# Attention by half a batch at a time ahead of and beside the first expert: float32 scores, normalised weights, one table of distances

## The chip, the cores and the metric

The kernel runs on one core of one Trainium2 chip. The metric is the device time of one execution, in microseconds (us), and less is better. Three timed runs of the kernel before took 1486.0, 1486.02 and 1492.36 us; the median is 1486.02 us.

## The reference, cut to what matters

Three layers follow one another, all in float32: attention with 2 batches, 8 heads, 768 positions and 64 elements a head; a mixture of 8 experts (1536 tokens, width 512, hidden width 1024) whose gates are normalised 8 times over rows and columns (the Sinkhorn steps); and a gated layer of hidden width 1536.

```python
def _attn_ref(q, k, v, n_global, n_local):      # n_global = 8, n_local = 96
    scores = scale * np.matmul(q, k.transpose(0, 1, 3, 2))
    rel = pos[:, None] - pos[None, :]
    is_global = pos[None, :] < int(n_global)
    is_local = (rel >= 0) & (rel < int(n_local))
    keep = is_global | is_local
    dist = np.where(is_global & ~is_local, float(n_local), np.abs(rel))
    bias = -slopes[:, None, None] * dist[None, :, :]
    scores = np.where(keep, scores + bias, -1e9)
    scores = scores - np.max(scores, axis=-1, keepdims=True)
    a = np.exp(scores)
    a = a / (np.sum(a, axis=-1, keepdims=True) + 1e-09)
    return np.matmul(a, v)

def _moe_ref(x, w_gate, w1, w2):
    P = np.exp(x @ w_gate - max)
    for _ in range(8):
        P /= P.sum(1, keepdims=True) + 1e-09
        P /= P.sum(0, keepdims=True) + 1e-09
        P *= N / E
    for e in range(E):
        out += P[:, e:e + 1] * (np.maximum(x @ w1[e], 0.0) @ w2[e])
```

## The kernel before, in words

Every large product is made of three products in the type float32r: a number is split into a high part and the rest (`xh` and `xl`, `wh` and `wl`, `hh` and `hl`), and high times high, high times rest and rest times high are added up in PSUM. Splitting a piece of weights takes one copy on ScalarE (L191, the high part) and one subtraction on GpSimd (L192, the rest).

Attention works on an item: one pair of heads and one block of 128 queries, against 256 keys (32 copied global keys, the 96 keys before the block and its own 128). There are 2 batches times 4 pairs times 6 blocks, 48 items. For an item TensorE makes the scores (L853; three float32r products for each head, with the heads in rows 0 to 63 and 64 to 127 of the array), VectorE adds a table of the head's biases and takes the minimum (L865), ScalarE takes the exponential (L870), two items later TensorE transposes the weights (L883) and ScalarE copies them out of PSUM (L884), and one item after that TensorE multiplies them with the values in float32 (L897, L901). The values have a 65th column of ones, so the row sums come out beside the result; VectorE divides by them (L729 to L733), and TensorE transposes the result (L719) into `xh` and `xl`. GpSimd copies the global keys and values into the blocks (L859, L906) and makes the tables of biases (L802, L807).

The program is generated in the order in which each engine runs it. Up to 97.2 us it emits the items of batch 0 (and the first steps of batch 1's), with the split of the first weights beside them. Bfloat16 products of zeros (`fill`, L657) stand ahead of and among the first items. Then come the visits of expert 0. A visit is one quarter of the hidden width, and runs one unit for each chunk of 3 blocks of tokens: the first product (two parts, f = 0 and 1, of 12 matmuls each), and then the second products of the unit before (3 blocks, 6 matmuls each). After each part and each block a tick is called, which emits some steps of a list that is spread evenly over the ticks (`Paced`). In the 4 visits of batch 0, of two units each, the list holds the items of batch 1. In the 4 visits of batch 1 it holds the gates with the 8 Sinkhorn steps, and the sums of halves of x that the experts 1 to 7 need (`trans_steps`). The weights of visit n+1 are split in the last unit of visit n. PSUM banks 2, 3, 6 and 7 are shared in turn by transposes and expert products in the visits of batch 0.

Of the kernel before, what the change touches and what calls it, by code (L numbers as in the profile page):

```python
# [9 lines left out]
F32 = mybir.dt.float32  # L10
F32R = mybir.dt.float32r
# [16 lines left out]
WAIT = 3  # L28
LAG = 2
TURN = (4, 4)  # L30
# [36 lines left out]
def tile_global_local_attention__then__sinkhorn_moe__then__glu(  # L67
# [86 lines left out]
    NB0 = NQ  # L154
    F0 = 2 * NB0
# [49 lines left out]
    def split_steps(n):  # L205

        vis = visits[n]
        steps = []
        if vis["kind"] == "moe":
            if vis["load"]:  # L210
                r = raw[vis["raw"]][:, 0 : 4 * FQ]
                steps += split_halves(r, wh[vis["slot"]][0], wl[vis["slot"]][0])
                steps += second_steps(n)
                steps.append(lambda b=vis["raw"]: load(b))
            return steps
# [11 lines left out]
    def split(n):  # L227
        for step in split_steps(n):
            step()
# [190 lines left out]
    def unit_second(n, t, at, j):  # L420
# [4 lines left out]
        if vis["kind"] != "glu":  # L425
            if n in (0, NB0):
# [184 lines left out]
    with tc.tile_pool(name="attn", bufs=1) as ap:  # L611
# [7 lines left out]
        qr = [ap.tile([P, NB, P], F32, name=f"qr{i}") for i in range(2)]  # L619
        kr = [ap.tile([P, NB, P], F32, name=f"kr{i}") for i in range(2)]  # L620
        vo = [ap.tile([P, NB, 2, D1], F32, name=f"vo{i}") for i in range(2)]

        def load_qk(s, blocks=slice(0, NB)):
            load_heads(s, ((qr, q), (kr, k)), blocks)

        def load_vo(s, blocks=slice(0, NB)):
            load_heads(s, ((vo, v),), blocks)

        def load_heads(s, pairs, blocks):
            if s >= B * NP:  # L630
                return
            b, p = divmod(s, NP)
# [701 lines left out]
```

## Time and profile before

| what | us |
|---|---|
| median of three runs | 1486.02 |
| the profiled execution's own time | 1493.77 |
| its span, from the first to the last instruction | 1492.0 |
| TensorE busy | 1465.4 (98%) |
| VectorE busy | 859.7 (58%) |
| ScalarE busy | 499.6 (33%) |
| GpSimd busy | 523.9 (35%) |
| mean granted TensorE clock | 0.984 |

The span lies 1.8 us inside the execution's own time. Matmuls overlap one another, so a busy TensorE is not a full one: what a group of matmuls costs is read from the starts of what stands in a row. The chain that ended last runs through TensorE for 95% of the span. Of the 40 slices of 37.3 us, the first two show granted clocks of 8 and 7 tenths, and all others 9 tenths or more.

### The profile page before, as it was taken

The page shows a single profiled execution, that of the slowest core. Times are in us where ns is not written, and L with a number is a line of the kernel's source. Part 1 is how long each engine was busy: PE and PEld are TensorE (multiplying, and loading weights), DVE is VectorE, ACT ScalarE, POOL GpSimd, SP SyncE. Part 2 cuts the span into 40 slices and gives each one's busy share as a digit, 9 for nine tenths or more (in the row PEclk, how much of TensorE's full clock was granted, in tenths as well). Part 3 has the DMA queues.
Part 4 walks back from the last instruction along what each step waited for, and adds up shares of the span by engine and source line. Part 5 has one row for each costly group of instructions (what it writes and reads, how often), then busy time and mean ns, then how long its engine had stood idle before and what let it go on. Part 6 is the DMA issues. An engine that isn't in the chain of part 4 may idle for free.

```text
span 1492.0 us, 19772 instructions
## 1 busy us (share of the span) xinstructions
PE 1465.4 (98%) x7427; PEld 1282.4 (86%) x7427; DVE 859.7 (58%) x1587; ACT 499.6 (33%) x1064; POOL 523.9 (35%) x604
## 2 busy tenths in 40 slices
PE   8999998899999999999999999999999999999998
PEld 6888877789998999989999999899998888888887
DVE  4455437867666657666666666667665533333323
ACT  4554422333333333333333333333333331122111
POOL 3312103454444444445345445344452211121110
PEclk8799999999999999999999999999999999999999
DMA  7232100122122122121222122121220100010002
GB/s 163 65 93 57 50 2 21 37 74 90 50 71 72 62 88 71 50 71 58 91 71 71 50 71 99 51 71 50 71 85 29 43 29 29 29 43 29 0 1 85
DMA packets 83605, 87.33 MB, mean 59 GB/s; under 512 B 41264, under 2 KB 58672, under 8 KB 83504
## 3 DMA queue, kind: packets, MB, share of 16 engines
q1 hardware_dynamic: 83216, 86.01, 18.5%
q8 instruction: 59, 0.97, 0.3%
q14 instruction: 42, 0.34, 0.1%
q10 hardware_dynamic: 288, 0.00, 0.0%
HBM read 73.42 MB, written 12.58 MB: 58 GB/s over the span
## 4 chain that ended last, share of the span: by engine, by line
PE 95%; DVE 2%; POOL 1%; issue 1%; ACT 1%; DMA 1%; SPq 0%; DVEq 0%; ACTq 0%; POOLq 0%
PE bank L354 29%; PE bank L356 29%; PE bank L355 29%; PE bank L853 2%; PE bank L901 1%; PE bank L883 1%; PE bank L897 1%; PE bank L708 1%; POOL wl L192 0%; PE bank L719 0%; DMA work<-in_moe_w_gate_dram 0%; PE bank L1282 0%; DMA lens<-in_n_local_dram 0%; DVE work L1122 0%; DVE csum L1207 0%
## 5 line engine op out<-in xcount | busy, mean ns | idle before, releaser
L437 DVE SCALAR_TENSOR_TENSOR acc<-bank,gate,acc 128x512 f32<-128x512 f32 x336 | 251.8, 749 | 232.9 <-PE bank L356 230.0
L354 PE MATMUL bank<-wh,hh 128*128 128x512 f32 x912 | 360.8, 396 | 0.0
L356 PE MATMUL bank<-wh,hl 128*128 128x512 f32 x912 | 360.0, 395 | 0.0
L355 PE MATMUL bank<-wl,hh 128*128 128x512 f32 x912 | 358.2, 393 | 0.0
L192 POOL TENSOR_TENSOR wl<-raw,wh 128x512 fp32r<-128x512 f32 (+1 forms) x188 | 201.8, 1089 | 378.4 <-ACT wh L191 370.3
L354 PE MATMUL bank<-xh,wh 128*128 128x384 f32 (+1 forms) x720 | 255.5, 355 | 5.4 <-DVE kept L539 3.0
L356 PE MATMUL bank<-xh,wl 128*128 128x384 f32 (+1 forms) x720 | 252.9, 351 | 0.0
L355 PE MATMUL bank<-xl,wh 128*128 128x384 f32 (+1 forms) x720 | 251.7, 350 | 0.0
L356 PEld LDWEIGHTS bank<-wh,hl 128*128 128x128 f32 x912 | 171.4, 188 | 38.7
L354 PEld LDWEIGHTS bank<-wh,hh 128*128 128x128 f32 x912 | 171.7, 188 | 27.2
L355 PEld LDWEIGHTS bank<-wl,hh 128*128 128x128 f32 x912 | 171.6, 188 | 26.7
L529 ACT ACTIVATE hh<-kept 128x384 fp32r<-128x384 f32 x168 | 88.1, 525 | 314.5 <-DVE kept L539 314.5
L354 PEld LDWEIGHTS bank<-xh,wh 128*128 128x128 f32 x720 | 137.0, 190 | 19.2 <-DVE kept L539 3.3
L355 PEld LDWEIGHTS bank<-xl,wh 128*128 128x128 f32 x720 | 136.8, 190 | 13.4 <-DVE xl L1287 0.5
L356 PEld LDWEIGHTS bank<-xh,wl 128*128 128x128 f32 x720 | 136.3, 189 | 5.7
L192 POOL TENSOR_TENSOR wl<-work,wh 128x256 fp32r<-128x256 f32 x112 | 93.4, 835 | 94.3 <-ACT wh L191 94.3
L543 ACT ACTIVATE kept<-bank 128x384 f32<-128x384 f32 x168 | 82.4, 491 | 122.7 <-PE bank L356 122.7
L531 DVE SCALAR_TENSOR_TENSOR hl<-kept,hh 128x384 fp32r<-128x384 f32 x168 | 115.3, 687 | 0.4 <-ACT hh L529 0.3
L356 PE MATMUL bank<-th,wl 128*128 128x384 f32 x336 | 113.0, 336 | 0.0
L354 PE MATMUL bank<-th,wh 128*128 128x384 f32 x336 | 112.5, 335 | 0.1
L355 PE MATMUL bank<-tl,wh 128*128 128x384 f32 x336 | 112.4, 335 | 0.0
L412 DVE TENSOR_TENSOR z<-bank,sg 128x512 f32<-128x512 f32 x36 | 24.9, 692 | 139.3 <-PE bank L356 139.3
(151 smaller groups left out, 1908.9 us busy)
## 6 DMA issues: line engine op xcount, KB each, us to landing
raw<-in_moe_w_dram SPq DMA_DIRECT2D x68, 512.0 KB, 4.3
glw<-work SPq DMA_DIRECT2D x36, 256.0 KB, 2.3
raw<-glw SPq DMA_DIRECT2D x18, 512.0 KB, 3.2
work<-in_moe_w_gate_dram SPq DMA_DIRECT2D x12, 512.0 KB, 3.9
work<-in_moe_w_val_dram SPq DMA_DIRECT2D x12, 512.0 KB, 3.9
work<-in_moe_w_out_dram SPq DMA_DIRECT2D x12, 512.0 KB, 3.8
out_dram<-o SPq DMA_DIRECT2D x12, 256.0 KB, 2.0
qr<-in_q_dram SPq DMA_DIRECT2D x14, 192.0 KB, 4.2
```

Source lines behind the costliest of these rows:

```text
L192: nc.gpsimd.tensor_tensor(out=lo, in0=r, in1=h.bitcast(F32), op=ALU.subtract)
L354: nc.tensor.matmul(lhsT=ah, rhs=bh, start=first, stop=False, **mm)
L355: nc.tensor.matmul(lhsT=ah, rhs=bl, start=False, stop=False, **mm)
L356: nc.tensor.matmul(lhsT=al, rhs=bh, start=False, stop=end, **mm)
L412: nc.vector.tensor_tensor(out=z, in0=ps, in1=sg, op=ALU.mult)
L437: nc.vector.scalar_tensor_tensor(out=a, in0=ps, scalar=gate[:, t, e : e + 1], in1=a, op0=ALU.mult, op1=ALU.add,)
L529: nc.scalar.activation(out=hh[:, f, :C], in_=src, func=AF.Relu)
L531: lambda: nc.vector.scalar_tensor_tensor(out=hl[:, f, :C], in0=src, scalar=0.0, in1=hh[:, f, :C].bitcast(F32), op0=ALU.max, op1=ALU.subtract,)
L543: nc.scalar.activation(out=snap[:, i], in_=ps, func=AF.Copy)
L708: nc.tensor.transpose(ps[:, j * P : (j + 1) * P], src[:, 3 * g + j, :], ident)
L853: nc.tensor.matmul(out=ps[j][:, lo:KW], lhsT=qT[rows, a, own], rhs=kT[rows, c, keys], start=(n == 0), stop=(n == 2),)
L883: nc.tensor.transpose(ps[:, j, a, :], e[:, j, a * P : (a + 1) * P], ident)
```

## The change

Attention is done by units of half a batch and one pair of heads (3 items). Only the 4 units of the first half of batch 0 stand ahead of the visits. The visits of batch 0 are now 8, of one unit each: four for the first half, and four, in the other order of the quarters, for the second half. The list beside them holds the items from the second half of batch 0 on. The 4 visits of batch 1 follow with two units each, as before. The weights are loaded and split in 8 visits instead of 6, and a visit's first weights are split after its predecessor's second weights and that load, so they stand last in the unit before.

In an item the scores are one float32 product for each head. The queries are scaled by the head's slope on the way in, so that one table of distances serves all heads. The sums of the weights come from the exponential's instruction; VectorE takes their reciprocals, and GpSimd multiplies the weights of the first head and VectorE those of the second, before the transposes. The values then stand still in the array (64 columns for each head) and the weights move through it, so that x comes out transposed, and the division and the transposes behind it are gone. One `fill` matmul follows each of the first 12 items, four each of the first three. The 8 additions of high part and rest in `trans_steps` go from VectorE to GpSimd. The branch for other lengths (not run here) loads for itself.

```diff
@@ the visits
-    for f in range(NQ):
-        visits.append(dict(kind="moe", e=0, f=f, chunks=halves[0], slot=f % 2, load=True))
-    for n, f in enumerate(reversed(range(NQ))):
-        slot = f % 2 if n < 2 else 1 - n % 2
-        visits.append(dict(kind="moe", e=0, f=f, chunks=halves[1], slot=slot, load=n >= 2))
+    up, down = list(range(NQ)), list(reversed(range(NQ)))
+    for order, over in (
+        (up, halves[0][:1]), (down, halves[0][1:]), (down[2:] + up[2:], halves[1])
+    ):
+        for n, f in enumerate(order):
+            again = len(visits) >= NQ and n < 2
+            visits.append(
+                dict(
+                    kind="moe", e=0, f=f, chunks=over, slot=len(visits) % 2 ^ (len(visits) >= NQ),
+                    load=not again, start=n == 0,
+                )
+            )
...
-    NB0 = NQ
-    F0 = 2 * NB0
+    NB0 = CB * NQ
+    F0 = NB0 + NQ
@@ the split of weights
+    def first_steps(n):
+        vis = visits[n]
+        if vis["load"]:
+            r = raw[vis["raw"]][:, 0 : 4 * FQ]
+            yield from split_halves(r, wh[vis["slot"]][0], wl[vis["slot"]][0])
+
+    def ahead_steps(n):
+        if visits[n]["load"]:
+            yield from second_steps(n)
+            yield lambda b=visits[n]["raw"]: load(b)
+        if n + 1 < F0:
+            yield from first_steps(n + 1)
@@ run_visit
-        per = chunks[0][1] + (2 if visits[n]["kind"] == "moe" else 4)
-        ahead = Paced(ahead, per * (len(chunks) - 1) * PACE // 12)
+        at = 0 if visits[n]["kind"] == "moe" else 1
+        per = chunks[0][1] + (4 if at else 2)
+        ahead = Paced(ahead, per * (len(chunks) - at) * PACE // 12)
         side = tick
         def tick():
             side()
-            if u:
+            if u >= at:
                 ahead.tick()
@@ an item
-                for n, (a, c) in enumerate(((0, 0), (0, 1), (1, 0))):
-                    for j in range(2):
-                        rows = slice(j * D, (j + 1) * D)
-                        nc.tensor.matmul(
-                            out=ps[j][:, lo:KW], lhsT=qT[rows, a, own], rhs=kT[rows, c, keys],
-                            start=(n == 0), stop=(n == 2),
-                        )
+                for j in range(2):
+                    rows = slice(j * D, (j + 1) * D)
+                    nc.tensor.matmul(
+                        out=ps[j][:, lo:KW], lhsT=qT[rows, own], rhs=kT[rows, keys],
+                        start=True, stop=True,
                     )
...
                     nc.vector.tensor_tensor_reduce(
-                        out=e[:, j, lo:KW], in0=ps[j][:, lo:KW], in1=bm, scale=1.0, scalar=3.0e38,
+                        out=e[:, j, lo:KW], in0=ps[j][:, lo:KW], in1=dst0 if i == 0 else dst,
+                        scale=SLOPES[2 * p + j], scalar=3.0e38,
                         op0=ALU.add, op1=ALU.min, accum_out=mn[:, j : j + 1],
                     )
                 for j in range(2):
                     nc.scalar.activation(
                         out=e[:, j, lo:KW], in_=e[:, j, lo:KW], func=AF.Exp, scale=-1.0,
-                        bias=mn[:, j : j + 1],
+                        bias=mn[:, j : j + 1], accum_out=rs[:, j : j + 1],
                     )
...
+            def normalised(w):
+                e, rs = live[w]
+                lo = NG + NW if work[w][1] == 0 else 0
+                nc.vector.tensor_scalar(out=rs, in0=rs, scalar1=EPS, scalar2=None, op0=ALU.add)
+                nc.vector.reciprocal(out=rs, in_=rs)
+                for j, eng in enumerate((nc.gpsimd, nc.vector)):
+                    eng.tensor_scalar(
+                        out=e[:, j, lo:KW], in0=e[:, j, lo:KW], scalar1=rs[:, j : j + 1],
+                        scalar2=None, op0=ALU.mult,
+                    )
...
-                for j in range(2):
-                    o = ps[:, ((i % 3) * 2 + j) * D1 : ((i % 3) * 2 + j + 1) * D1]
-                    if i > 0:
+                for a in range(0 if i > 0 else 1, 2):
+                    for j in range(2):
                         nc.tensor.matmul(
-                            out=o, lhsT=aT[:, j, 0, :], rhs=vo[s % 2][:, i - 1, j, :],
-                            start=True, stop=False,
+                            out=ps[j * D : (j + 1) * D, i % UB * P : (i % UB + 1) * P],
+                            lhsT=vo[p][:, i - 1 + a, j, :], rhs=aT[:, j, a, :],
+                            start=(a == 0 or i == 0), stop=(a == 1),
                         )
...
+                if i % UB == UB - 1:
+                    tok = slice(b * S + g * C, b * S + (g + 1) * C)
+                    nc.scalar.activation(out=xh[:, p, tok], in_=ps, func=AF.Copy)
+                    nc.vector.tensor_tensor(
+                        out=xl[:, p, tok], in0=ps, in1=xh[:, p, tok].bitcast(F32), op=ALU.subtract
                     )
@@ the order of the items
+                    yield lambda w=w: scores(w)
+                    if w < UB * NP:
+                        yield lambda w=w: fill(FILL if w <= LAG else 1)
+                    if ahead:
+                        yield ahead.pop(0)
+                if 0 <= w - 1 < n:
+                    yield lambda w=w - 1: normalised(w)
                 if 0 <= w - LAG < n:
-                    yield lambda x=work[w - LAG]: turned(*x)
+                    yield lambda w=w - LAG: turned(w)
                 if 0 <= w - LAG - 1 < n:
...
+                    yield lambda w=w - LAG - 1: values(w)
+                    if w - LAG - 1 == UB * NP - 1:
+                        yield None
...
-                side = Paced(steps[first_batch + 1 :], 5 * CB * NQ - 3)
+                side = Paced(steps[begin + 1 :], 5 * NB0 - 3)
                 for n in range(NB0):
-                    run_visit(n, side.tick, split_steps(n + 1))
+                    run_visit(n, side.tick, ahead_steps(n))
@@ trans_steps
         def whole(out, k, half):
             h, lo = block(k, half)
-            return lambda: nc.vector.tensor_tensor(
+            return lambda: nc.gpsimd.tensor_tensor(
                 out=out, in0=h.bitcast(F32), in1=lo.bitcast(F32), op=ALU.add
             )
```

On TensorE an item beside the visits of batch 0 stood like this (rows that only repeat are left out; `kr` and `e` are transposed, `aT` are the transposed weights, `vo` the values, `qT` and `kT` queries and keys):

```order
L708 MATMUL bank_70<-ident,kr_119 128x128 x3
L883 MATMUL bank_65<-ident,e_207 128x128 x4
L897 MATMUL bank_67<-vo_120,aT_214 128x65
L901 MATMUL bank_67<-vo_120,aT_214 128x65
...
L853 MATMUL bank_63<-kT_203,qT_201 128x256
L853 MATMUL bank_64<-kT_203,qT_201 128x256
...
```

And of the change, with the end of the fifth tick of the second visit and the first matmuls of the third:

```order
L884 MATMUL bank_65<-ident,e_228 128x128 x4
L898 MATMUL bank_68<-aT_239,vo_123 64x128 x4
L846 MATMUL bank_63<-kT_225,qT_221 128x256
L846 MATMUL bank_64<-kT_225,qT_221 128x256
L365 MATMUL bank_66<-xh,wh_78 128x384
L366 MATMUL bank_66<-xl,wh_78 128x384
L367 MATMUL bank_66<-xh,wl_82 128x384
```

Two scores stand where there were six, and four products with the values of 128 columns where there were four of 65; the third visit's first matmul, which reads the weights `wh_78` and `wl_82`, comes straight behind an item's scores.

On ScalarE, the split of the first weights `wh_78` for the third visit, and the first copy of that visit's result (`hh`), stood like this before (`e` is the exponential):

```order
L191 ACTIVATE wh_78<-raw_86 128x512
L392 ACTIVATE hh_76<-bank_69 128x384
L870 ACTIVATE e_206<-e_206,mn_210 128x256 x2
L191 ACTIVATE wh_78<-raw_86 128x512
L822 ACTIVATE qT_202<-bank_65 128x384
L884 ACTIVATE aT_214<-bank_66 128x512
L191 ACTIVATE wh_79<-raw_86 128x512
L870 ACTIVATE e_207<-e_207,mn_211 128x256 x2
L822 ACTIVATE qT_202<-bank_70 128x384
L191 ACTIVATE wh_79<-raw_86 128x512
L884 ACTIVATE aT_213<-bank_66 128x2x128
L392 ACTIVATE hh_76<-bank_69 128x384
```

And of the change:

```order
L830 ACTIVATE kT_225<-bank_69 128x384
L199 ACTIVATE wh_78<-raw_86 128x512
L885 ACTIVATE aT_238<-bank_65 128x512
L907 ACTIVATE xh<-bank_68 128x384
L860 ACTIVATE e_227,rs_235<-e_227,mn_231 128x256 x2
L199 ACTIVATE wh_78<-raw_86 128x512
L403 ACTIVATE hh_76<-bank_66 128x384
```

The second half of the first weights stood seven rows ahead of the visit's first copy, and now stands just ahead of it, behind the exponentials of the last item before the visit.

On GpSimd the first subtractions in the visits of batch 1 stood like this before (`tl` and `xl` are rests of the sums of halves of x, `wl` of weights):

```order
L192 TENSOR_TENSOR tl<-work,th 128x2x384 x2
L192 TENSOR_TENSOR wl_84<-raw_86,wh_80 128x512
L192 TENSOR_TENSOR tl<-work,th 128x2x384
L192 TENSOR_TENSOR wl_84<-raw_86,wh_80 128x512
L192 TENSOR_TENSOR wl_85<-raw_86,wh_81 128x512
```

And of the change:

```order
L1116 TENSOR_TENSOR work<-xh,xl 128x768 x4
L200 TENSOR_TENSOR tl<-work,th 128x2x384 x2
L200 TENSOR_TENSOR wl_84<-raw_86,wh_80 128x512
L200 TENSOR_TENSOR tl<-work,th 128x2x384
L200 TENSOR_TENSOR xl<-work,xh 128x2x384
L1116 TENSOR_TENSOR work<-xh,xl 128x768
L200 TENSOR_TENSOR wl_84<-raw_86,wh_80 128x512
L1116 TENSOR_TENSOR work<-xh,xl 128x768 x2
```

Eight additions of 768 columns have joined GpSimd's row, four ahead of the first subtraction and four among the later ones.

## Rows read from the trace of the kernel before

**Rows 1.** Busy time by stretch: length, then each engine's busy time (instructions), granted TensorE clock, DMA.

```profile
9.50:23.30 13.80, 11.48 (x86) 8.08 (x86) 8.57 (x33) 8.47 (x20) 6.23 (x12) 1.00 1.14 266
23.30:40.40 17.10, 17.10 (x87) 15.78 (x87) 6.69 (x29) 8.13 (x19) 7.50 (x16) 0.50 0.43 94
40.40:60.90 20.50, 18.04 (x157) 15.74 (x156) 11.43 (x46) 14.76 (x34) 11.31 (x22) 1.00 0.42 88
60.90:77.90 17.00, 17.00 (x87) 15.52 (x86) 7.03 (x27) 7.21 (x17) 1.76 (x7) 0.50 0.13 29
77.90:97.20 19.30, 18.84 (x168) 16.68 (x167) 11.60 (x48) 13.47 (x32) 2.89 (x11) 1.00 0.63 153
97.20:203.80 106.60, 106.09 (x706) 94.94 (x704) 50.62 (x147) 47.05 (x102) 21.85 (x38) 1.00 0.13 38
203.80:299.20 95.40, 83.39 (x397) 71.81 (x398) 65.77 (x128) 25.81 (x50) 32.77 (x26) 0.93 0.08 23
```

**Rows 2.** Timeline of TensorE: start, duration, line, operation, count.

```profile
12.59 1.04 PE L657 MATMUL bank<-zeros 128*128 128x512 bf16 x4
...
42.90 0.62 PE L853 MATMUL bank<-kT,qT 64*128 64x256 f32 x6
43.45 0.66 PE L883 MATMUL bank<-ident,e 128*128 128x128 f32 x4
43.95 0.33 PE L897 MATMUL bank<-vo,aT 128*128 128x65 f32 x2
...
44.79 0.82 PE L719 MATMUL bank<-ident,xsb 128*128 128x128 f32 x6
45.54 0.55 PE L853 MATMUL bank<-kT,qT 64*128 64x128 f32 x6
...
57.20 0.62 PE L853 MATMUL bank<-kT,qT 64*128 64x256 f32 x6
```

**Rows 3.** TensorE's groups from 97.2 to 203.8 us: busy time, mean ns of one.

```profile
L354 PE MATMUL bank<-xh,wh 128*128 128x384 f32 x64 | 22.9, 358 | 0.0
L354 PE MATMUL bank<-wh,hh 128*128 128x512 f32 x42 | 18.5, 439 | 0.0
L901 PE MATMUL bank<-vo,aT 128*128 128x65 f32 x84 | 15.6, 273 | 0.0
L853 PE MATMUL bank<-kT,qT 64*128 64x256 f32 x90 | 9.3, 312 | 0.0
L853 PE MATMUL bank<-kT,qT 64*128 64x128 f32 x18 | 1.7, 288 | 0.0
```

**Rows 4.** ScalarE's and VectorE's groups, 40.4 to 60.9 us; GpSimd's, 0 to 97.2 us.

```profile
L870 ACT ACTIVATE e<-e,mn 128x256 f32<-128x256 f32 x14 | 6.4, 501 | 4.8 <-DVE mn L865 4.7
L884 ACT ACTIVATE aT<-bank 128x512 f32<-128x512 f32 x8 | 4.7, 583 | 0.0
L831 ACT ACTIVATE kT<-bank 128x384 fp32r<-128x384 f32 x3 | 1.4, 469 | 0.0
L191 ACT ACTIVATE wh<-raw 128x512 fp32r<-128x512 f32 x2 | 1.2, 618 | 0.0
L865 DVE CUSTOM_DVE_ANT_0 e<-bank,bm 128x256 f32<-128x256 f32 x14 | 5.4, 420 | 1.2 <-PE bank L853 1.1
L192 POOL TENSOR_TENSOR wl<-raw,wh 128x512 fp32r<-128x512 f32 x4 | 5.1, 1269 | 6.4 <-ACT wh L191 6.4
```

**Rows 5.** TensorE's waits from 97 to 320 us: total, times, longest.

```profile
PE bank L1198 <- DVE gate L1192: 9.5, 2, 4.9
```

**Rows 6.** Timelines of VectorE and GpSimd: a Sinkhorn step alone, and one beside GpSimd; one addition.

```profile
262.47 0.95 DVE L1117 TENSOR_TENSOR work<-xh,xl 128x768 f32<-128x768 f32 x1
267.02 0.17 DVE L1207 TENSOR_SCALAR csum<-csum 128x8 f32<-128x8 f32 x1
274.54 1.69 DVE L1207 TENSOR_SCALAR csum<-csum 128x8 f32<-128x8 f32 x1
...
274.40 1.79 POOL L192 TENSOR_TENSOR tl<-work,th 128x768 fp32r<-128x768 f32 x1
```

More of the change, by code (lines that the diff above doesn't have):

```diff
@@ L205, in split_steps @@
     def split_steps(n):
[L207 to L215, printed above, removed]
+        vis, steps = visits[n], []
         for j, part in enumerate(glu_weights(vis)):
@@ L225, in glu_weights @@
         return g, v, (wh[vis["slot"]][1], wl[vis["slot"]][1])
-    def split(n):
-        for step in split_steps(n):
-            step()
     def form(i):
@@ new lines, in banded_tables @@
+            vec.scalar_tensor_tensor(
+                out=dst0, in0=dst0, scalar=nl, in1=far0, op0=ALU.add, op1=ALU.add
+            )
+            vec.tensor_scalar(
+                out=far[:, 0:NG], in0=gm[:, 0:NG], scalar1=-most, scalar2=most,
+                op0=ALU.mult, op1=ALU.add,
+            )
+            vec.tensor_scalar(
+                out=dst[:, 0:NG], in0=far[:, 0:NG], scalar1=nl, scalar2=None, op0=ALU.add
+            )
+            vec.tensor_scalar(
+                out=far[:, NG:KW], in0=lm, scalar1=-most, scalar2=most, op0=ALU.mult, op1=ALU.add
+            )
@@ new lines, in values @@
+                if 0 < i < NB - 1:
+                    nc.gpsimd.tensor_copy(out=vo[p][0:NG, i], in_=vo[p][0:NG, 0])
+                if i % UB == UB - 1:
[3 more added lines that the diff above has]
+                        out=xl[:, p, tok], in0=ps, in1=xh[:, p, tok].bitcast(F32), op=ALU.subtract
+                    )
+                    if b + 1 < B and g == CB - 1:
+                        for half in range(CB):
+                            load_v(b + 1, half, p)
@@ L911, in banded_steps @@
+            work = [(u, units[u][1] * UB + i) for u in range(len(units)) for i in range(UB)]
             n = len(work)
             ahead = list(prep(0))
-            bias = []
-            for j in (0, NB // 3 - 1):
-                yield ahead.pop(j)
+            for _ in range(2):
+                yield ahead.pop(0)
                 yield lambda: fill(FILL)
-            for h in range(2):
-                yield from banded_bias(t, h)
-            for w in range(n + LAG + 1 + TURN[-1]):
+            for w in range(n + LAG + 1):
@@ L920, in banded_steps @@
                 if w < n:
-                    s, i = work[w]
-                    if i == 0 and s < B * NP - 1:
-                        ahead += prep(s + 1)
-                        if s < NP - 1:
-                            bias = [x for h in range(2) for x in banded_bias(t, 2 * (s + 1) + h)]
-                    yield lambda s=s, i=i: scores(s, i)
-                    if w < LAG:
-                        yield lambda: fill(FILL)
-                    if i >= 1:
-                        for todo in (ahead, bias):
-                            for _ in range(-(-len(todo) // (NB - i))):
-                                yield todo.pop(0)
+                    u, i = work[w]
@@ L935, in banded_steps @@
                 if 0 <= w - LAG - 1 < n:
-                    s, i = work[w - LAG - 1]
-                    yield lambda s=s, i=i: values(s, i)
-                    if i == NB - 1:
-                        def loads(s=s):
-                            load_vo(s + 2)
-                        yield loads
-                for g in range(NB // 3):
-                    at = w - LAG - TURN[g]
-                    if 0 <= at < n and work[at][1] == NB - 1:
-                        s = work[at][0]
-                        yield list(finish_steps(s, lambda s=s: live["x", s]))[g]
-                        if s == NP - 1 and g == NB // 3 - 1:
-                            yield None
+                    yield lambda w=w - LAG - 1: values(w)
@@ L1233, in tile_global_local_attention__then__sinkhorn_moe__then__glu @@
     for n in range(NB0, F0 - 1):
-        run_visit(n, both, split_steps(n + 1))
+        run_visit(n, both, ahead_steps(n))
     other.finish()
     n = F0 - 1
-    ahead = [*sum_steps(F0), *(lambda i=i: form_step(F0, i) for i in range(4)), *second_steps(F0)]
+    ahead = [
+        *ahead_steps(n), *sum_steps(F0), *(lambda i=i: form_step(F0, i) for i in range(4)),
+        *second_steps(F0),
+    ]
     run_visit(n, side.tick, ahead)
```

252 lines of the change are left out of this document (110 added, 142 removed).

## The prediction

> **What bounds the kernel now.** I read the chain of waits first: TensorE carries 95% of the span, so only time on TensorE's path counts. The table by stretch [rows 1] then says where that engine has slack. From 9.5 to 97.2 us it runs attention alone; in two stretches, 17.1 and 17.0 us long, the granted clock is 0.50, that is 1.2 instead of 2.4 GHz. It was at full clock before each of them and was given attention alone there. There it starts 87 instructions in 17.1 us (5.1 a us) and at full clock 157 in 20.5 us (7.7 a us), so the two stretches cost a third of 34.1 us, 11.4 us. From 97.2 to 203.8 us TensorE is busy for 106.09 of 106.6 us with VectorE at 50.6, ScalarE at 47.1 and GpSimd at 21.9: dense, and paid by TensorE's work. From 203.8 to 299.2 us 12 us of TensorE are open, 9.5 of them two waits for VectorE's gates [rows 5], and the clock is 0.93. What lies behind 299.2 us is not touched.
>
> **An item on TensorE.** By starts in a row [rows 2], an item costs 0.55 for the scores (42.90 to 43.45), 0.50 for four transposes, 0.84 for the values (43.95 to 44.79), and 0.75 for six transposes of x, 0.125 each and one an item. Two transposes of queries and keys make 0.25. Sum 2.27 us; alone at full clock the pace is (57.20 - 42.90) / 6 = 2.38. In the visits of batch 0 there are 108 score matmuls, six an item, so 18 items' scores, and 84 matmuls of line 901, four an item, so 21 items' values [rows 3]; taken as 19.7 items they are 44.7 us. The other 61.9 us are 318 expert matmuls, three times 64 and three times 42, 0.2 us each.
>
> The change makes one float32 product of each head's scores; the trace shows such a product as two matmuls (84 for 21 items and two heads). None of 256 columns stands in it. A transpose of 128 columns costs 0.125, so I take 0.25 for each of the four. In a row that is 1.0; with the heads wholly beside each other, as the six of before run in 0.55, it is 0.5. Only the middle two can pair, since each head's two stand together: 0.75, or +0.20 an item (-0.05 to +0.45). The values become eight matmuls of 128 columns, each filling half the array: 1.0 in a row, 0.5 in pairs. I take pairs that overlap only in part and one more change of shape, 0.70, or -0.14 (-0.34 to +0.16). The transposes of x go, -0.125. Together -0.07 an item (-0.5 to +0.5), so 2.2 beside the visits. A rule bears on this: the Trainium skill, TensorEngine Tiling (Array Packing), section Key Properties, says that different tiles can load and multiply in parallel, but that a change of tiling drains the engine. For rows the trace agrees (six scores in 0.55 us); no run here shows column tiles, and by the rule alone the values would cost 0.5 and each change of shape something more.
>
> **Ahead of the visits.** The order has 15 score steps and the values of 12 items there, instead of 30 and 27. TensorE's pace is 2.38 - 0.07 + 0.26 for a fill (four took 1.04, [rows 2]) = 2.57 us. ScalarE has two exponentials at 0.50, a copy of the transposed weights at 0.58, two thirds of a copy at 0.47 for queries and keys, and a third of one for x [rows 4], 2.05 us, and the summing in the exponentials, which no row shows (nothing, or up to another 0.2 each). With two engines so close I take 2.7 an item, and 2.2 for each of the first three, which have four fills but little else. 9.5 + 6.6 + 12 x 2.7 = 48.5 us instead of 97.2: **-48.7**. [...]
>
> **Beside the visits of batch 0.** The expert work is the same 318 matmuls, and 34.7 items (33 scores, 36 values) stand beside it: 61.9 + 34.7 x 2.2 = 138.2 instead of 106.6: **+31.6**. Per item VectorE has two minima at 0.42, a reciprocal, a product and part of a difference, about 2 us, and ScalarE about 2.3, against 3.7 us of TensorE a tick, so both hide, as the two added sets of weights do: each is four splits of 0.62 on ScalarE and 1.27 on GpSimd [rows 4].
>
> **The visits' first weights.** Here a wait is added. The last half of a visit's first weights is split at the fifth of five ticks, on ScalarE behind the exponentials of the item whose scores stand just ahead of the visit; no expert matmul is between. Counted from the end of these scores: two minima 0.9, the second exponential 0.5, the split 0.62, GpSimd's subtraction 1.27, together 3.3 us. TensorE has eight matmuls at 0.2 before it needs this rest, 1.6 us: a wait of 1.7. All engines' queues behind it stand still for as long, since the visit's first copies wait for these matmuls. It comes at the third, fourth, seventh and eighth visit, 6.8 us. The first visit has no second products and so two ticks only; three splits pile up behind its last tick: 1.4 for minima and exponential, 0.47 and 0.58 for two copies, 0.62 for a split that isn't needed yet, then two subtractions of 1.27, 5.6 us, against 1.3 of cover (transposes 0.9, two matmuls): 4.3. Together **+11.1**. Two visits of batch 1 split first weights in the same place, but without attention on ScalarE: 1.2 each, **+2.4**. If ScalarE is early, all this is nothing; if it is an item late, it is 3.7 more each time.
>
> **The visits of batch 1.** VectorE loses eight additions of 0.95, 7.6 of its 65.8 us; GpSimd gains as many of about 1.8. The two waits for the gates, 9.5 us with a clock loss of 7% of 95.4 (6.7 us), can vanish (-16) or come once or twice more (+8 each). I take **-2**, near no change, since GpSimd is as near the chain as VectorE (below).
>
> **The sum.** -48.7 + 31.6 + 11.1 + 2.4 - 2 = -5.6 us on the profiled execution, 1493.77 us, which stands 7.75 above the median of the three runs and near the slowest. I put the same difference on the median: 1486.0 - 5.6, **1480.4 us**, with 1473 to 1488 for this case alone. About 0.5% (7.4 us) is what a measurement of this kernel can tell from no change.
>
> **The rivals.**
> - *The splits are early and TensorE never waits at a visit.* 13.5 us less, 1467. For it: ScalarE is busy for 47.1 of 106.6 us beside the visits now. Against: the order, which puts the split behind the exponentials.
> - *The clock falls ahead of the visits as it does now.* One stretch of 17 us at 0.50 costs a third, 5.7: 1486. For it: it fell twice under items of the same kind; against: the fills, and that the stage ends at 48.5 us.
> - *The values' halves do not run beside each other.* 1.0 instead of 0.70, 0.3 x 48 items = 14: 1495. For it: nothing in the trace shows halves of the columns; against: the halves of the rows do.
> - *The first weights come too late (slower).* ScalarE is a whole item late, because its copy of the transposed weights waits for TensorE, which waits in turn: 4 us at seven visits instead of 13.5 in all, +14.5, and waits of that length come with a fallen clock (6.7 us for 9.5 of waits now); if half of them do, +10: 1505. It decides from about 3.8 us a visit: 27 us of waits make the whole slower by over 0.5%.
> - *GpSimd holds up VectorE.* One Sinkhorn instruction on VectorE took 0.17 us alone and 1.69 us beside a subtraction on GpSimd, and both ended together [rows 6]. The eight additions on GpSimd can each add some 1.5 us to the chain of gates, 12 in all; if the ticks cover half and the clock takes its part, TensorE loses 6 + 4 instead of gaining 2: 1492. The Trainium skill, SBUF — State Buffer, section Who interferes with whom, states the rule: the two engines share a port pair, and whoever comes second waits for the other's whole instruction if VectorE's has two inputs in SBUF or a two-port mode. The trace agrees, with the 1.69.
>
> **How the numbers follow.** Chances: the forecast 0.36, splits early 0.27, clock 0.12, halves 0.07, weights late 0.10, port 0.08. Faster by over 0.5%, below 1478.6: 0.15 of the forecast's 0.36, all of the second, 0.01 of the third: 0.43. Slower, above 1493.4: 0.02, 0.04, 0.09 and 0.02 of the last four: 0.17. The rest, 0.40, is no change. The range of 1462 to 1500 takes in all but the late weights and the far ends of an item's bounds.
>
> **What would show it.** TensorE's first expert matmul at 47 to 50 us with a clock of 1.00; if it comes at 54 or later, the clock or ScalarE's load was misjudged. The eighth visit over at about 198 us. In the list of waits, line 367 on the weights' rests of line 200 at five visits, 11 us in all; none there makes the first rival right. An item's scores at 0.75 and values at 0.70 by starts; the values at 1.0 would mean that halves don't pair. The waits for the gates still near 9.5 us. I am wrong as a whole if TensorE stays busy throughout and the time yet stands above 1488: then an item costs more than its parts.

## The result, and the profile after

The changed kernel takes **1500.16 us** (median of 12 runs, 1498.5 to 1503.35), the kernel before 1487.17 on the same chip (12 runs, 1484.49 to 1495.76). The ratio is **1.0077**, 95% interval 1.0059 to 1.0095: slower, by 13.0 us. Forecast were 1480.4, that is 5.6 below the kernel before; it came out 13.0 above, so the difference is missed by 18.6 us, and the time lies just above the range's upper end of 1500.

I cut both traces at three instructions: the first expert product, the first expert product behind the attention, and the first product of the experts 1 to 7. In the trace of before these stand at 97.2, 206.1 and 299.3 us (the span that [rows 1] gives as 97.2 to 203.8, and the tail up to the next expert product).

| stage | before | after | measured | forecast |
|---|---|---|---|---|
| ahead of the visits | 97.2 | 45.7 | -51.5 | -48.7 |
| visits of batch 0, up to the next expert product | 108.9 | 159.4 | +50.5 | +31.6 + 11.1 |
| visits of batch 1 | 93.2 | 98.2 | +5.0 | +2.4 - 2 |
| all behind | 1192.7 | 1193.9 | +1.2 | 0 |
| span | 1492.0 | 1497.2 | +5.2 | -5.6 |

Busy time by stretch of the changed kernel: length, each engine's busy time (instructions), the granted clock, DMA. The first three lines are the stages that answer to [rows 1], the others three stretches of 10 us at visits' starts.

```profile
9.50:45.70 36.20, 30.65 (x235) 18.88 (x236) 21.62 (x108) 27.92 (x91) 18.85 (x34) 1.00 0.71 164
45.70:205.10 159.40, 140.99 (x915) 103.63 (x915) 77.57 (x284) 86.12 (x238) 71.76 (x102) 0.94 0.26 68
205.10:303.30 98.20, 86.73 (x398) 74.58 (x399) 56.51 (x117) 25.27 (x48) 46.11 (x34) 0.90 0.08 22
...
50.00:60.00 10.00, 5.84 (x34) 4.53 (x33) 2.39 (x10) 5.58 (x16) 7.54 (x8) 0.85 0.19 53
80.00:90.00 10.00, 7.22 (x37) 5.52 (x38) 2.56 (x12) 4.43 (x13) 3.53 (x7) 0.83 0.21 48
100.00:110.00 10.00, 8.00 (x44) 5.93 (x43) 3.46 (x16) 3.97 (x12) 3.38 (x7) 0.83 0.35 88
```

Beside batch 0 TensorE was busy for 106.09 of 106.6 us before [rows 1], or of 108.9 with the tail; now, the tail counted in, 18.4 of 159.4 us are open, and the clock is 0.94. TensorE's waits of the changed kernel (total, times, longest) say for what: the first four lines are from 45.7 to 205.1 us, the last two from there to 303.3 us, where they answer to [rows 5].

```profile
PE bank L365 <- ACT wh L199: 8.7, 5, 2.7
PE bank L367 <- POOL wl L200: 4.5, 5, 1.4
PE bank L365 <- issue: 3.2, 1, 3.2
PE bank L898 <- POOL vo L904: 1.2, 2, 0.8
...
PE bank L1197 <- DVE gate L1191: 6.7, 2, 3.5
PE bank L367 <- POOL wl L200: 4.8, 2, 2.4
```

The first two lines are the visits' first weights: 13.2 us, at the five visits that the forecast named: 4.2 at the second, 2.9 at the third, 2.0 to 2.1 at the fourth, seventh and eighth. The third is the tail: between the last attention product and the next expert product nothing is left to run beside it. One such wait, at the third visit of the changed kernel, by engine (start, duration, line, operation, count, idle time before):

```profile
77.86 0.70 PE L846 MATMUL bank<-kT,qT 64*128 64x256 f32 x4
78.49 0.44 PE L365 MATMUL bank<-xh,wh 128*128 128x384 f32 x1
...
79.55 0.34 PE L367 MATMUL bank<-xh,wl 128*128 128x384 f32 x1
81.98 0.44 PE L365 MATMUL bank<-xh,wh 128*128 128x384 f32 x1 [2.10 <-ACT wh L199]
...
83.41 0.44 PE L367 MATMUL bank<-xh,wl 128*128 128x384 f32 x1 [0.80 <-POOL wl L200]
...
80.83 0.49 ACT L860 ACTIVATE e<-e,mn 128x256 f32<-128x256 f32 x1
...
81.31 0.61 ACT L199 ACTIVATE wh<-raw 128x512 fp32r<-128x512 f32 x1
...
77.62 1.27 DVE L869 TENSOR_SCALAR rs<-rs 128x2 f32<-128x2 f32 x1
...
79.86 0.41 DVE L854 CUSTOM_DVE_ANT_0 e<-bank,dst 128x256 f32<-128x256 f32 x1
80.20 0.42 DVE L854 CUSTOM_DVE_ANT_0 e<-bank,dst 128x256 f32<-128x256 f32 x1
...
85.41 0.16 DVE L869 TENSOR_SCALAR rs<-rs 128x2 f32<-128x2 f32 x1
...
77.60 1.27 POOL L200 TENSOR_TENSOR wl<-raw,wh 128x512 fp32r<-128x512 f32 x1 [1.81 <-ACT wh L199]
...
82.08 1.27 POOL L200 TENSOR_TENSOR wl<-raw,wh 128x512 fp32r<-128x512 f32 x1 [1.65 <-ACT wh L199]
```

The same two ends of the chain at the seventh visit, the first product, right behind the scores, and the two that wait:

```profile
156.24 0.44 PE L365 MATMUL bank<-xh,wh 128*128 128x384 f32 x1
...
158.84 0.45 PE L365 MATMUL bank<-xh,wh 128*128 128x384 f32 x1 [1.29 <-ACT wh L199]
...
160.24 0.44 PE L367 MATMUL bank<-xh,wl 128*128 128x384 f32 x1 [0.78 <-POOL wl L200]
```

The chain is the forecast one: scores, minima, second exponential, split, subtraction. But it starts late. At 77.62 VectorE adds a constant to two columns, which takes 0.16 us alone (at 85.41); here it takes 1.27 us, beside a subtraction of 1.27 us on GpSimd, and both end together. So the minima start at 79.86, 1.3 us after the scores. From the scores' end (78.49) to the product that reads the rest (83.41) it takes 4.9 us instead of the 3.3 of the forecast; at the seventh visit, where VectorE has no such row, 4.0 (156.24 to 160.24). TensorE's cover is the eight matmuls of the forecast: six before it waits for the second half of the high part, and two more before it waits for the rest.

An item on TensorE of the changed kernel, which answers to [rows 2]:

```profile
151.50 0.66 PE L898 MATMUL bank<-aT,vo 128*64 128x128 f32 x8
152.08 0.70 PE L846 MATMUL bank<-kT,qT 64*128 64x256 f32 x4
152.72 0.55 PE L827 MATMUL bank<-ident,kr 128*128 128x128 f32 x3
...
154.49 0.60 PE L884 MATMUL bank<-ident,e 128*128 128x128 f32 x4
155.02 0.66 PE L898 MATMUL bank<-aT,vo 128*64 128x128 f32 x8
```

By starts the values take 0.58 us, the scores 0.64, four transposes 0.53; forecast were 0.70, 0.75 and 0.50.

### The profile page after: what moved, and what is told of

Its sections match the earlier page's. It is cut to its first block, busy times and chain, and to the rows that moved or that the text cites. A ratio compares the mean times of both kernels' runs of the same rounds, so it can differ in the third digit from the quotient of the medians.

```text
span 1497.2 us, 19809 instructions
## 1 busy us (share of the span) xinstructions
PE 1452.5 (97%) x7293; PEld 1242.3 (83%) x7296; DVE 853.1 (57%) x1639; ACT 514.0 (34%) x1168; POOL 577.1 (39%) x650
## 4 chain that ended last, share of the span: by engine, by line
PE 91%; POOL 3%; issue 2%; DVE 2%; ACT 1%; DMA 1%; SPq 0%; DVEq 0%; ACTq 0%; POOLq 0%
PE bank L367 29%; PE bank L365 29%; PE bank L366 28%; PE bank L846 2%; PE bank L898 2%; POOL wl L200 1%; PE bank L884 1%; ACT e L860 1%; POOL tl L200 1%; PE bank L827 1%; DVE e L854 0%; DMA work<-in_moe_w_gate_dram 0%; PE bank L1284 0%; DMA lens<-in_n_local_dram 0%; ACT wh L199 0%
## 5 line engine op out<-in xcount | busy, mean ns | idle before, releaser
L200 POOL TENSOR_TENSOR wl<-raw,wh 128x512 fp32r<-128x512 f32 (+1 forms) x196 | 210.6, 1089 | 370.8 <-ACT wh L199 365.2
L365 PE MATMUL bank<-xh,wh 128*128 128x384 f32 (+1 forms) x720 | 259.3, 360 | 16.1 <-ACT wh L199 8.7
L367 PE MATMUL bank<-xh,wl 128*128 128x384 f32 (+1 forms) x720 | 256.7, 356 | 9.3 <-POOL wl L200 9.3
```

Of the source, the lines that this page charges most:

```text
L200: nc.gpsimd.tensor_tensor(out=lo, in0=r, in1=h.bitcast(F32), op=ALU.subtract)
L365: nc.tensor.matmul(lhsT=ah, rhs=bh, start=first, stop=False, **mm)
L367: nc.tensor.matmul(lhsT=al, rhs=bh, start=False, stop=end, **mm)
```

## The experiments

**Was the trace of before a usual one?** Its own time, 1493.77, was 7.75 above the median it was put on. Two runs of the kernel before, unchanged, each a single execution.

> The kernel before, unchanged, profiled once more. Theory A (the trace of before that the prediction rests on is one of the slower executions, since its time, 1493.77, lies 7 us above the median of 12 runs, 1487.17): the two stretches at a granted clock of 0.50 between 9.5 and 97 us, which cost 11.4 us there, are fewer or shorter where the time is near 1487; then the gain of 11.4 us that the sum took from them is not to be had against the median. Theory B (the clock pattern is the same in all executions, and the profile itself costs the 7 us): two stretches of some 17 us again, first expert matmul at 97 us, whatever the time.

Measured: 1488.68 us, span 1486.9. Stretches of this trace:

```profile
9.50:89.20 79.70, 73.17 (x576) 62.11 (x576) 44.81 (x181) 51.48 (x120) 29.58 (x66) 0.94 0.59 132
89.20:198.20 109.00, 106.19 (x707) 95.05 (x705) 51.80 (x150) 47.65 (x103) 21.91 (x39) 1.00 0.13 37
```

> The kernel before, unchanged, for a third profile of the stage ahead of the visits. Theory 'the clock there differs from execution to execution, and the one that the prediction was worked out from was among the worst': first expert matmul at 83 to 92 us, at most 20 us of half clock ahead of it, and a span under 1490 us. Rival 'two stretches of 17 us at half clock are the rule': first expert matmul at 96 us or later, span 1491 us or more.

Measured: 1484.42 us, span 1482.6. Stretches of this trace:

```profile
9.50:86.10 76.60, 70.02 (x578) 59.13 (x577) 44.79 (x181) 51.44 (x120) 29.63 (x66) 0.98 0.62 137
86.10:195.50 109.40, 106.14 (x707) 95.00 (x705) 51.72 (x149) 47.58 (x103) 21.86 (x38) 1.00 0.13 37
```

The stage ahead of the visits ends at 89.2 and 86.1 us instead of 97.2, with a clock of 0.94 and 0.98; the visits take the same 109 us. So against these two the change gains 43.5 and 40.4 us ahead of the visits, not 51.5. The first theory of each expectation holds: 8 to 11 us of the gain belonged to the one execution that the prediction was worked out from.

**Late weights put into the kernel before.**

```diff
             if vis["load"]:
                 r = raw[vis["raw"]][:, 0 : 4 * FQ]
-                steps += split_halves(r, wh[vis["slot"]][0], wl[vis["slot"]][0])
                 steps += second_steps(n)
+                steps.append(no_tick)
+                steps += split_halves(r, wh[vis["slot"]][0], wl[vis["slot"]][0])
                 steps.append(lambda b=vis["raw"]: load(b))
```

> The kernel before with one thing of the change alone: a visit's second weights are split ahead of its first ones, so that the last half of the first weights is split at the last of the five ticks, as in the changed kernel. Theory A (the late first weights are what made the change slower): TensorE waits for line 192's rests and line 191's copies at the five visits that split weights, some 2 to 4 us each, 12 us in all, with short stretches of half clock behind them, so 10 to 18 us slower than before, 1.007 to 1.012. Theory B (the lateness matters only beside the heavier items of the change, where ScalarE and GpSimd do more): under 4 us slower.

Measured: 1492.50 us (10 runs), ratio 1.0035 (1.0018 to 1.0051). TensorE's waits of this run, first from 83.0 to 297.5 us, then up to 197.1 us alone, and its stretches, ahead of the visits and beside both batches:

```profile
PE bank L357 <- POOL wl L192: 6.6, 5, 2.4
...
PE bank L355 <- ACT wh L191: 2.3, 2, 1.5
...
PE bank L357 <- POOL wl L192: 1.9, 3, 0.8
PE bank L355 <- ACT wh L191: 0.7, 1, 0.7
```

```profile
9.50:83.00 73.50, 67.93 (x576) 57.64 (x576) 44.65 (x181) 51.13 (x120) 29.52 (x66) 1.00 0.65 143
83.00:197.10 114.10, 108.02 (x708) 94.79 (x706) 51.80 (x150) 47.69 (x103) 22.09 (x39) 1.00 0.12 36
197.10:297.50 100.40, 86.49 (x397) 73.94 (x398) 61.99 (x125) 25.30 (x48) 32.83 (x26) 0.89 0.06 22
```

There are 8.9 us of waits, where 12 were expected, and the median is 5 us above before: under the 10 to 18 of theory A and over the 4 of theory B, so neither holds as it stood. Beside batch 0 the waits are short, 0.8 us at most, and the clock stays at 1.00 (114.1 us, 5 more than before). In batch 1 they are up to 2.4 us, the clock is 0.89, and the stage takes 100.4 us, 7 more. So a late split is paid in the kernel before too, with 12 us in the two stages of this profile. That the median shows only 5 goes with the stage ahead of the visits, which ended at 83.0 us with a clock of 1.00, earlier than in all three profiles of the kernel before (86.1 to 97.2). The edit also turns the split that runs beside that stage; whether that helped there, or this was a fast execution, no run here shows.

**The order turned in the changed kernel.**

```diff
     def ahead_steps(n):
+        if n + 1 < F0:
+            yield from first_steps(n + 1)
         if visits[n]["load"]:
             yield from second_steps(n)
             yield lambda b=visits[n]["raw"]: load(b)
-        if n + 1 < F0:
-            yield from first_steps(n + 1)
```

> The changed kernel with a visit's first weights split ahead of the second weights and the load of the visit before (three lines in another order). The trace of the changed kernel shows 18.0 us of waits for first weights (9.3 for GpSimd's rests, 8.7 for ScalarE's copies), three short stretches of half clock behind them up to 108 us and two behind those in the visits of batch 1. Theory A (these waits and their clock are the loss): the waits go but for that at the second visit, 14 us, and some 7 us of clock with them, so 18 to 24 us faster than the changed kernel: 1476 to 1482, ahead of before by 5 to 11 us. Theory B (the items cost more than their parts, the waits only stand in for others, as for banks or for VectorE): under 8 us faster, still not ahead of before.

Measured: 1481.22 us (10 runs), ratio 0.9954 (0.9937 to 0.9971), 19 us below the changed kernel. But in batch 1 this order lets second products run ahead of the split of their weights (the next expectation says which): a wait that the work needs is left out, this version does not compute what the changed kernel does, and its time alone proves nothing. So the order was then turned beside batch 0 alone, where nothing of that kind happens:

```diff
     def ahead_steps(n):
+        one = len(visits[n]["chunks"]) == 1
+        if one and n + 1 < F0:
+            yield from first_steps(n + 1)
         if visits[n]["load"]:
             yield from second_steps(n)
             yield lambda b=visits[n]["raw"]: load(b)
-        if n + 1 < F0:
+        if not one and n + 1 < F0:
             yield from first_steps(n + 1)
```

> The changed kernel with the next visit's first weights split ahead of this visit's second weights in the eight visits beside batch 0 alone; the visits of batch 1 stay as in the changed kernel. (In the run first_early the order was turned in the visits of batch 1 too, and there the first tile's second product read half of its weights before they were split; this kernel computes what the changed kernel does.) Theory 'late first weights': the waits for first weights beside batch 0's visits fall from 14.5 us to under 7 us, the half clock behind them goes, the stage from the first expert matmul to the last attention matmul takes 139 to 143 us instead of 155.8, and the time is 1481 to 1485 us, ratio to before 0.996 to 0.999. Rival 'first_early was short because its second products had nothing to wait for': the waits go, but waits for second weights come in their place, and the time is 1490 us or more.

Measured: 1484.83 us (10 runs), ratio 0.9971 (0.9948 to 0.9993). Its stretches, and its waits from 45.5 to 188.7 us:

```profile
45.50:188.70 143.20, 133.48 (x914) 99.89 (x914) 78.82 (x284) 85.53 (x238) 70.98 (x103) 0.99 0.28 76
188.70:287.90 99.20, 84.88 (x397) 71.92 (x398) 58.05 (x117) 25.38 (x48) 46.00 (x34) 0.91 0.07 22
```

```profile
PE bank L368 <- ACT wh L199: 2.4, 2, 1.3
PE bank L370 <- POOL wl L200: 1.5, 2, 0.8
```

The waits for first weights fall from 13.2 to 3.9 us, the clock rises from 0.94 to 0.99, and the stage takes 143.2 instead of 159.4 us: one order of steps is worth 16.2 us there, and 15.3 us on the median. The stage of batch 1, left as it was, stays long (99.2 and 98.2). The lines that are left are of first products (`xh,wh` and `xh,wl`); no second product waited, so that rival fell.

**How much of it is the clock?** The changed kernel with products of zeros where TensorE waits.

```diff
             for f in range(2):
+                if f == 0:
+                    state["hold"](n)
                 ps = state["A"].next()[:, :m]
...
+                def hold(n):
+                    for _ in range({1: 70, 2: 45, 3: 45, 6: 45, 7: 45}.get(n, 0)):
+                        nc.tensor.matmul(
+                            out=bank[4 + n % 2][:, C:512], lhsT=zeros[:, 0:P], rhs=zeros[:, 0:P],
+                            start=True, stop=True,
+                        )
```

> The changed kernel with bfloat16 products of zeros (128x128 by 128 columns, 70 ahead of the second visit's first product, 45 ahead of the third's, fourth's, seventh's and eighth's, into columns that nothing reads), about 0.054 us each at full clock, 3.8 and 2.4 us at a visit, so that TensorE works where it waits for the first weights. It splits the loss into waits and clock. Theory 'the waits bring the half clock, which costs 4 to 7 us of its own': the stretches at half clock behind the second to fourth visits go, the waits fall from 14.5 to 4 us or less, and the time is 1493 to 1497 us, 3 to 7 below the changed kernel's 1500.2. Rival 'the clock is a bystander': 1500 to 1503 us, since the fills only stand in the waits' place.

Measured: 1493.40 us (10 runs), ratio 1.0032 (1.0013 to 1.0051). Stretches of this run, the stage and the three starts of visits:

```profile
45.50:199.40 153.90, 147.18 (x1165) 113.73 (x1165) 77.68 (x284) 86.17 (x238) 71.63 (x103) 0.99 0.26 71
...
50.00:60.00 10.00, 9.53 (x107) 8.19 (x107) 2.29 (x9) 5.46 (x14) 7.55 (x8) 1.00 0.17 55
80.00:90.00 10.00, 9.23 (x66) 7.30 (x64) 4.49 (x17) 5.75 (x16) 4.97 (x7) 1.00 0.01 2
...
100.00:110.00 10.00, 10.00 (x72) 7.68 (x71) 4.67 (x18) 5.09 (x15) 3.92 (x6) 1.00 0.28 63
```

More work, and 6.8 us less time. TensorE spends the waits busily, and the clock stays at 1.00 where it was 0.83 to 0.85. In the stage it is 159.4 to 153.9, 5.5 us for the clock. The other 10.7 us down to 143.2 go with the waits themselves, of which early_split_one_chunk has 9.3 us less.

> The changed kernel, unchanged, for a second profile. Theory 'late first weights bring the half clock each time': the same five visits wait, 17 to 19 us in all, and at least three of them are followed by a stretch at half clock; the first expert matmul comes at 45.6 us and the span is 1495 to 1500 us. Rival 'the clock behind the visits is a chance of that one execution': no more than one such stretch, span under 1492 us.

Measured: 1501.74 us, span 1499.9. Its stage beside batch 0, and its waits for first weights there (from 45.8 to 206.3 us):

```profile
45.80:206.30 160.50, 142.00 (x915) 104.94 (x915) 77.69 (x284) 86.28 (x238) 71.72 (x102) 0.95 0.25 68
```

```profile
PE bank L365 <- ACT wh L199: 8.6, 5, 2.7
PE bank L367 <- POOL wl L200: 4.1, 5, 1.1
```

The same five visits wait, 12.7 us against 13.2 (16.9 with batch 1, where 17 to 19 were expected), four of them are followed by a half clock, and the stage's clock is 0.95 against 0.94. The loss is no chance of one execution.

**The additions on GpSimd**, put back on VectorE in the changed kernel (`nc.gpsimd.tensor_tensor` becomes `nc.vector.tensor_tensor`).

> The changed kernel with the eight additions of high part and rest back on VectorE. Theory A (GpSimd's additions do little: they delay GpSimd's splits of first weights in the visits of batch 1, two waits of 2.6 us, and spare VectorE 7.6 us; both are small): within 4 us of the changed kernel. Theory B (the port that GpSimd and VectorE share makes them the cause of the loss in the visits of batch 1, which take 98.2 us instead of 93.2): 5 to 9 us faster than the changed kernel.

Measured: 1498.22 us (6 runs), ratio 1.0068 (1.0042 to 1.0094). The waits for the gates in this run, from 0 to 330 us:

```profile
PE bank L1197 <- DVE gate L1191: 8.6, 3, 5.0
```

8.6 us, against 6.7 in the changed kernel's first profile and 8.7 in its second: 2 us here are within what one kernel does by itself. The time is within the interval of the changed kernel's, 2 us below it; theory A holds. The eight additions decide nothing that shows.

**What is left: the tail, and batch 1.** On early_split_one_chunk the attention's last steps end two ticks earlier, and in batch 1 the raw load stands behind the first weights' split.

```diff
         if visits[n]["load"]:
             yield from second_steps(n)
-            yield lambda b=visits[n]["raw"]: load(b)
+            if one:
+                yield lambda b=visits[n]["raw"]: load(b)
         if not one and n + 1 < F0:
             yield from first_steps(n + 1)
+        if not one and visits[n]["load"]:
+            yield lambda b=visits[n]["raw"]: load(b)
...
-                side = Paced(steps[begin + 1 :], 5 * NB0 - 3)
+                side = Paced(steps[begin + 1 :], 5 * NB0 - 5)
```

> The kernel early_split_one_chunk with two more edits: the attention's last steps are paced to end two ticks earlier (over 38 instead of 40 less 3 ticks becomes 40 less 5), so that the eighth visit has its second products beside the last item; and in the visits of batch 1 the raw load stands behind the split of the next first weights, which brings that split two ticks earlier. Theory 'what is left is the uncovered tail and two late splits': 3 to 4 us from the tail (198 to 205 us in the changed kernel), 2 to 5 from the splits and their clock, so 1475 to 1479 us, ratio 0.992 to 0.995. Rival 'the packed items make ScalarE late': more waits for first weights in the earlier visits, no gain against early_split_one_chunk, 1481 to 1485 us.

Measured: **1475.40 us** (5 runs), ratio to before **0.9904** (0.9865 to 0.9943). Stretches of this run:

```profile
45.50:186.40 140.90, 135.69 (x915) 101.91 (x916) 74.76 (x283) 85.47 (x238) 71.00 (x103) 0.98 0.28 75
186.40:279.40 93.00, 83.72 (x399) 71.95 (x398) 57.04 (x118) 25.28 (x48) 46.05 (x34) 0.93 0.08 27
```

The stage beside batch 0, with the tail, is 2.3 us shorter, and that of batch 1 6.2 us, back at the 93.2 us of before. The two edits were not run apart, so which of them gave what is argued from the stages. This version beats both kernels.

> The kernel early_split_and_tail with the eight additions of the weight split on VectorE again, as in the kernel before. Theory 'GpSimd's additions cost nothing where the splits are early': within 2 us of early_split_and_tail, 1474 to 1477 us. Rival 'GpSimd holds up VectorE at the gates': the waits for the gates fall by 3 us or more, and the time is 1469 to 1472 us.

Measured: 1473.28 us (4 runs), ratio 0.9911 (0.9888 to 0.9934): not to be told from early_split_and_tail. The waits for the gates are 9.0 us, against 6.9 there, not 3 us less, so the rival fell.

**The halves of the columns**, with the values of one head ahead of the other's in early_split_and_tail.

```diff
-                for a in range(0 if i > 0 else 1, 2):
-                    for j in range(2):
+                for j in range(2):
+                    for a in range(0 if i > 0 else 1, 2):
```

> The kernel early_split_and_tail with the values' matmuls in another order: both blocks of one head, then both of the other, instead of the two heads by turns, so that the halves of the array's columns stand next to each other only once an item. It tells what the pairing of column halves is worth, which the prediction could only bound. Theory 'the halves run beside each other when they stand side by side': the values of an item go from 0.59 to 0.9 to 1.0 us; 36 items beside the visits make 11 to 15 us, and the time is 1486 to 1491 us. Rival 'eight matmuls take what they take in either order' (no pairing, or the queue finds the pairs by itself): 1475 to 1478 us.

Measured: 1474.83 us (4 runs), ratio 0.9929 (0.9911 to 0.9946). Timeline of TensorE of this run:

```profile
152.89 0.67 PE L904 MATMUL bank<-aT,vo 128*64 128x128 f32 x8
153.49 0.44 PE L371 MATMUL bank<-xh,wh 128*128 128x384 f32 x1
```

0.60 us in this order too, and the same time: my theory fell. That the halves must stand next to each other was wrong. That they run beside each other is read from single records: in early_split_and_tail the eight start in pairs 6 to 7 ns apart, here 13 to 14 ns apart, one pair 0.1 to 0.15 us behind the other, where transposes of as many columns start 0.109 us apart one by one. The records do not say which half each fills; how the engine brings the pairs together from this order stays open.

## Why the prediction was wrong

- **The gain ahead of the visits was right, and measured against the wrong time.** 45.7 us and a clock of 1.00 were forecast as 48.5 and full. What failed is the step "I put the same difference on the median": the 97.2 us held two stretches of half clock [rows 1] that cost 11.4 us, and an execution near the median has them at most in part (before_again and before_third). Profiled before stands 6.6 us above the median of 12 runs, profiled after (1499.02) 1.1 below its own; with the 5.2 us of the spans that makes the 13.0. So 7.7 of the 18.6 us of the miss lie here. The other 10.8 lie between the spans (+5.2 for -5.6): -2.8 ahead of the visits, 7.8 beside batch 0, 4.6 in batch 1 and 1.2 behind. The prediction has both numbers, 11.4 and 7.75, and yet takes the gain whole.
- **The visits' first weights were mis-sized: 11.1 forecast, 13.2 measured, and 5.5 for the clock that the term left out.** Place and count were right, and the second visit's size (4.2 against 4.3). The other four waited 2.0 to 2.9 us instead of 1.7: the chain from the scores to the rest took longer than 3.3 us, 4.9 at the third, where VectorE started late, held by GpSimd's own split, and 4.0 at the seventh. The Trainium skill, SBUF — State Buffer, section Who interferes with whom, has the rule that if VectorE's instruction runs in a two-port mode or has two inputs in SBUF, whichever of the two engines issues first holds the shared ports for its whole instruction; the row of 1.27 us agrees with it, though no row names the mode. I had weighed this rule only for the eight additions, where whole_on_vector shows no cost.
- **An item was cheaper than forecast, which by luck hid part of the miss.** As an estimate, 159.4 less 61.9 of expert work, 13.2 and 6.2 of waits (tail, global values, and two of 1.0 and 0.8 for transposed and normalised weights) and 5.5 of clock leaves 72.6 us for 34.7 items, 2.09 instead of 2.2: 3.8 us less. The stage's miss, 159.4 against 138.2 + 11.1 + 2.3 of tail as before, is 7.8: 2.1 + 5.5 + 3.9 (6.2 less 2.3) - 3.8 = 7.7.
- **Batch 1: +0.4 forecast, +5.0 measured.** The two late splits wait 2.4 us each, not 1.2, 4.8 us in all, and the gain of 2 did not come as a whole: the gates wait 6.7 us (8.7 in after_again) instead of 9.5, but the clock is 0.90 instead of 0.93. early_split_and_tail takes the 5 us back, by an earlier split and an earlier tail together.
- **The rivals.** "The first weights come too late" has the right mechanism, waits and a fallen clock behind them, at a smaller price: 18.0 us of waits (13.2 and 4.8) instead of 28, since ScalarE was not a whole item late, and 5.5 for the clock beside batch 0 instead of 10. With early splits the time is 1475 to 1485, not 1467, from a sum whose gain was put some 8 us too high. "The halves do not run beside each other" is refuted by the records, "GpSimd holds up VectorE" at the gates by whole_on_vector and early_split_tail_vector, and the clock ahead of the visits did not fall.
- Not settled: which waits bring a half clock. In the profile of after it fell behind those at 56, 82 and 103 us (0.85, 0.83 and 0.83 in the stretches of 10 us), and not behind those of 2.0 us at the seventh and eighth visit; in after_again it fell behind the seventh and eighth too, and not behind the fourth.

## What to carry to other kernels

When work is cut into visits half as long, every step that is paced over a visit comes up twice as tight: ask which of the paced steps the next visit needs first, and emit that one first; here the order of two lists was worth 1% of the kernel. Count a wait on TensorE twice, once as time and once as a chance of half clock behind it. And before a difference is put on a median, ask whether the stage that shrinks is the one that made the profiled execution slow.

## What the runs showed of the hardware that was not expected

- Products of zeros in the place of waits made a kernel 6.8 us faster (1493.4 against 1500.16), with the clock of their stage at 0.99 instead of 0.94.
- Two float32 products into different halves of the array's columns start 6 to 8 ns apart, eight of them in 0.58 to 0.60 us; the Trainium skill, TensorEngine Tiling (Array Packing), section Key Properties, says that different tiles can load and multiply in parallel, and these records agree for columns. A change of shape costs little: four transposes of 0.109 us by their starts and the change to the values' shape take 0.53, so that about 0.09 is left for the change.
- A VectorE addition on 2 columns grew from 0.16 to 1.27 us beside a GpSimd subtraction of 1.27 us, ahead of the third visit and again, at 176.34 us, ahead of the eighth.
- The same program spent 97.2, 89.2 and 86.1 us on its first stage in three executions, with clocks of 0.81, 0.94 and 0.98.
